# Chunk-select attention into soft mixture of experts: the first pair's loads, the last weight and the output stores rearranged

## The chip, the core and the metric

The kernel runs on one core of a Trainium2 chip. The metric is the device time of one execution in microseconds, the median of three runs. A separate profiled execution gives the trace; its own time stands beside its span below.

The core has a matrix engine (PE, TensorE), a vector engine (DVE), a scalar engine (ACT), GpSimd (POOL) and SyncE (SP). Each works through its own instructions in the order in which the program lists them, and waits on semaphores for the others. Transfers are issued by GpSimd or SyncE here and carried out by 16 DMA engines.

## What is computed

Two stages, with B = 4, H = 8, S = 768, D = 64 (the reference, cut):

```python
# attention that keeps, for each query row, 6 of 24 chunks of 32 keys
k_min, k_max = k_chunks.min(3), k_chunks.max(3)
ub = sum(maximum(q * k_min, q * k_max), -1)          # bound per chunk
ub = where(causal, ub, -1e9)
sel = chunk of the key is among the top 6 of ub
attn = softmax(where(sel & causal, q @ k.T / 8, -1e9))
x = (attn @ v) as (3072, 512)

# soft mixture of experts: 8 experts of 4 slots, F = 1024
logits = x @ phi                                      # (3072, 32)
slot_input = softmax(logits, over rows).T @ x         # (32, 512)
slot_out[e] = relu(slot_input[e] @ w1[e]) @ w2[e]
out = softmax(logits, over slots) @ slot_out          # (3072, 512), fp32
```

## The kernel before

**Units of work.** The attention is done in 16 pairs of heads (4 per batch element), each of 768 rows. One pair goes through these helpers: `load` (line 140) brings k and q, 192 KB each in bf16, by a GpSimd DMA that casts from the fp32 in memory; `load_v` (147) does the same for v. `transposes` (199) turns k or q with 12 small matmuls into a PSUM tile, which `evac_T` (211) copies out by ScalarE as kT or qT. `kmin` and `kmax` (220, 226) reduce the chunks on VectorE, `qsplit` (236) makes the negative and positive parts of q (for pair 0 the positive part is a ScalarE relu, line 241), `ubound` (246) multiplies them into the chunk bounds, and `select` (263) finds the sixth largest bound and marks the chunks below it (`ns`, not selected; one small copy by GpSimd at line 270). `ns_transposes` and `evac_ns` turn the marks. `scores` (290) then accumulates kT x qT and, from the constant `smask` and the turned marks, a large negative penalty; `expo` (314) is ScalarE's exponential, six per pair; `mask` (327) clears the causal triangle on GpSimd; `pv` (336) multiplies with v, and `normalise` (354) divides into x. `x_transposes` and `evac_x` turn x for the logits.

**The experts' side.** After every fourth pair (one batch element) the `moe_` helpers (385 to 496) compute logits with phi, a running maximum over rows, the dispatch product accumulated in `si_acc`, and the combine weights, kept turned in `cT_all`. The 16 weights of 1 MB in bf16 (w1 of expert e is number e, w2 is 8 + e) come by `load_w` (130), one GpSimd DMA each, cast from fp32. `wplan` (508) says in which pair's iteration `weights` (511) issues how many; number 0 is issued at 546, number 15 in the iteration of pair 15.

**Order.** There is no planner: each engine does its work in the order in which the lines are written, and the tile pools hand out buffers in rotation and insert the waits. PSUM tiles come from three pools with the tags "sc", "tp" and "at".

**The start** (156 to 192 and 517 to 568). VectorE clears constants, GpSimd issues k and q of pair 0, builds the identity, then builds `squad`, loads pair 1, builds `qgrp` and `caus`, and loads pair 2. VectorE adds `schunk` from `squad` (187) and ScalarE expands it to `smask` (188). PE runs `warm` (194), matmuls of 512 columns on ones whose result nobody reads: 9 before the transposes of the first k, 3 before those of q, then 2, 2 and 5. Pair 0's scores follow. phi and the second identity `identf` (fp32) are issued at 544 and 545 on GpSimd, ahead of weight 0. The loop over the other pairs is at 570; in it k and q of pair i + 4 are loaded at 595, v of pair i + 2 at 622, and the weights by 624 (or 575 for later ones, whose pools open there).

**The end.** GpSimd clears `siT_pad` and `hT_pad` (689, 690) and sets `zrow` (740) to ones. The slot sums are added into `siT_pad` and `zrow` on VectorE (743, 750). `experts_in` (762) and `relu` (772) give the hidden layer, `hidden_T` (775) turns it, `sums` (784) inverts the sums. `experts_out` (795) multiplies with w2 into two PSUM tiles, one for each column half y of 256; expert 7, the last weight, comes last: 8 matmuls for y = 0, then ScalarE's scaled copy `so_sb0` (847), 4 for y = 1, `half_out(0, 0)`, 4 more, and `so_sb1` (851), also ScalarE. The output is 12 row pairs m of 256 rows (two rows per partition, x = 0 and 1). `half_out` (827) does the first two row pairs by column halves: a product into a PSUM tile of its own for each x, `scaled` (821) by VectorE for x = 0 and by ScalarE for x = 1, and SyncE stores of 128, 128, 256, 256 and 256 KB, in which each partition's row piece has 1 KB. The loop at 857 does row pairs 2 to 11 whole (rows m of both x: 4 KB per partition, 512 KB per store, the last in two of 256 KB). Its PSUM tiles are separate for x = 0 and x = 1 and rotate over "at, sc, tp, sc, tp", and its five `o_sb` buffers are freed by the stores.

## Time and profile before

| | us |
|---|---|
| median of 3 runs | 166.47 (165.97 to 166.54) |
| profiled execution, its own time | 166.89 |
| its span in the trace | 165.2 |
| PE busy | 142.8 (86%) |
| ScalarE busy | 122.8 (74%) |
| VectorE busy | 119.9 (73%) |
| GpSimd busy | 103.1 (62%) |

The DMA engines moved 32.94 MB in the span, 199 GB/s on the mean. Besides, the exponentials of line 321 (96 of them, 83.1 us) are the largest group of ScalarE and the causal masks of line 331 (96, 38.4 us) that of GpSimd.

How to read what follows. The timeline lists runs of instructions on one engine: start, duration in us, engine, source line, operation, output<-inputs and shape, count, and in brackets the idle time before it with what ended that. PEld is PE's weight load. The page's rows by 40 slices give a busy share in tenths per slice, or the GB/s moved. A DMA row gives the size and the us from issue to landing. A row of waits names the waiting engine, line and tile, what it waited for, and total us, number of times and the longest. "Before" and "after" are times from the start of the span.

### The profile page before, as it was taken

To read this page: it belongs to the slowest core of one execution; us is meant where nothing else is said; L and a number is where in the kernel's file an instruction comes from. 1 tells how busy PE (TensorE), PEld (TensorE's weight loads), DVE (VectorE), ACT (ScalarE), POOL (GpSimd) and SP (SyncE) were. 2 spreads that over 40 slices of the span, in tenths; PEclk is the share of its full clock that TensorE was granted. 3 is DMA by queue.
4 is the path that set the end of the run, shared out by engine and by line. 5 is a ranking of instruction groups with operands and counts; after the bars stand their busy time and mean duration, and the time that the engine had idled before them with its cause. 6 is when DMAs were issued, how large, how long until landed. Compare 5 with 4: busy or idle time off the path is not lost.

```text
span 165.2 us, 6132 instructions
## 1 busy us (share of the span) xinstructions
PE 142.8 (86%) x2541; PEld 97.6 (59%) x2541; DVE 119.9 (73%) x419; ACT 122.8 (74%) x166; POOL 103.1 (62%) x202
## 2 busy tenths in 40 slices
PE   7986779999999898999999899998989999894500
PEld 2353456766767585677768567675868747552200
DVE  3376988989999979989997999898536521083620
ACT  3668879999999798999989699996886311193510
POOL 6978749979889398878949796768936200000000
PEclk9999999999999999999999999999999999999655
DMA  3999999999999999999999999999999999158995
GB/s 46 148 157 171 207 157 106 171 192 201 203 200 204 201 205 181 211 193 183 209 191 212 193 214 193 208 219 197 203 207 217 211 215 192 28 195 326 408 404 197
DMA packets 41132, 32.94 MB, mean 199 GB/s; under 512 B 26384, under 2 KB 35600, under 8 KB 41104
## 3 DMA queue, kind: packets, MB, share of 16 engines
q0 software_dynamic: 38416, 26.25, 108.0%
q1 hardware_dynamic: 2688, 6.29, 9.9%
q8 instruction: 20, 0.33, 0.7%
q14 instruction: 8, 0.07, 0.1%
HBM read 52.49 MB, written 6.29 MB: 356 GB/s over the span
## 4 chain that ended last, share of the span: by engine, by line
PE 31%; DMA 29%; ACT 18%; DVE 9%; issue 5%; POOL 4%; DVEq 0%; ACTq 0%
DMA w_sb<-in_moe_w_dram 14%; ACT e_sb L321 11%; DMA k_in<-in_k_dram 9%; DMA out_dram<-o_sb 6%; PE sc_ps L297 6%; PE at_ps L349 4%; PE tr_ps L205 4%; PE sc_ps L307 4%; PE warm_ps L197 4%; ACT qT L214 4%; PE xT_ps L371 2%; DVE mx L268 2%; PE ub_ps L256 2%; DVE x_sb L362 1%; POOL e_sb L331 1%
## 5 line engine op out<-in xcount | busy, mean ns | idle before, releaser
L321 ACT ACTIVATE e_sb<-sc_ps 128x1024 bf16<-128x1024 f32 (+1 forms) x96 | 83.1, 917 | 8.1 <-PE sc_ps L307 7.7
L331 POOL TENSOR_SCALAR_AFFINE_SELECT e_sb<-e_sb 128x256 bf16<-128x256 bf16 x96 | 38.4, 419 | 16.2 <-ACT e_sb L321 15.6
L297 PE MATMUL sc_ps<-qT,kT 64*128 64x384 bf16 (+3 forms) x258 | 36.8, 305 | 2.7 <-ACT e_sb L321 1.7
L307 PE MATMUL sc_ps<-nsT,smask 64*128 64x384 bf16 (+2 forms) x294 | 38.1, 284 | 0.1
L349 PE MATMUL at_ps<-v_t,e_sb 128*128 128x65 bf16 x672 | 29.9, 194 | 1.2 <-DVE x_sb L362 1.0
L349 PEld LDWEIGHTS <-e_sb 128*128 128x128 bf16 x672 | 25.4, 98 | 3.6 <-issue 2.1
L268 DVE MAX8 mx<-ub_ps 128x8 f32<-128x8 f32 (+1 forms) x192 | 17.0, 165 | 4.9 <-PE ub_ps L256 4.1
L297 PEld LDWEIGHTS <-kT 64*128 64x128 bf16 x258 | 14.0, 93 | 10.8 <-issue 5.4
L150 POOL DMA_DIRECT2D v_t<-in_v_dram x16 | 16.9, 1053 | 0.7 <-PE ns_ps L279 0.5
L307 PEld LDWEIGHTS <-smask 64*128 64x128 bf16 x294 | 14.9, 94 | 3.8 <-issue 0.6
L223 DVE TENSOR_REDUCE mm<-kT 128x24 bf16<-128x768 bf16 x16 | 15.1, 943 | 2.5 <-ACT kT L214 2.5
L362 DVE TENSOR_TENSOR x_sb<-at_ps,inv 128x768 bf16<-128x768 f32 (+1 forms) x17 | 15.5, 910 | 0.6
L229 DVE TENSOR_REDUCE mm<-kT 128x24 bf16<-128x768 bf16 x16 | 15.1, 943 | 0.0
L214 ACT COPY qT<-tr_ps 128x768 bf16<-128x768 bf16 x16 | 12.8, 800 | 2.5 <-PE tr_ps L205 2.5
L214 ACT COPY kT<-tr_ps 128x768 bf16<-128x768 bf16 x16 | 12.8, 801 | 1.5 <-PE tr_ps L205 1.5
L145 POOL DMA_DIRECT2D k_in<-in_k_dram x16 | 11.7, 734 | 1.1 <-POOLq L885 0.8
L145 POOL DMA_DIRECT2D q_in<-in_q_dram x16 | 11.5, 722 | 0.0
L138 POOL DMA_DIRECT2D w_sb<-in_moe_w_dram x16 | 11.4, 716 | 0.0
L382 DVE COPY xT_sb<-xT_ps 128x768 bf16<-128x768 bf16 (+1 forms) x15 | 8.1, 537 | 3.2 <-PE xT_ps L371 3.2
L863 PE MATMUL o_ps<-so_sb,cT_all 128*128 128x256 bf16 x40 | 6.8, 298 | 3.8 <-DVE o_sb L823 3.5
L205 PE MATMUL tr_ps<-ident,k_in 128*64 128x128 bf16 x192 | 8.7, 229 | 1.1 <-DMA k_in<-in_k_dram 1.1
L256 PE MATMUL ub_ps<-bd,qpn 128*128 128x48 bf16 x192 | 7.8, 183 | 1.3 <-DVE qpn L239 0.9
(125 smaller groups left out, 212.1 us busy)
## 6 DMA issues: line engine op xcount, KB each, us to landing
w_sb<-in_moe_w_dram POOLq DMA_DIRECT2D x16, 1024.0 KB, 14.0
out_dram<-o_sb SPq DMA_DIRECT2D x9, 512.0 KB, 5.3
k_in<-in_k_dram POOLq DMA_DIRECT2D x16, 192.0 KB, 7.0
q_in<-in_q_dram POOLq DMA_DIRECT2D x16, 192.0 KB, 7.3
v_t<-in_v_dram POOLq DMA_DIRECT2D x16, 192.0 KB, 8.5
out_dram<-oh_sb SPq DMA_DIRECT2D x3, 256.0 KB, 4.2
out_dram<-o_sb SPq DMA_DIRECT2D x2, 256.0 KB, 4.8
out_dram<-oh_sb SPq DMA_DIRECT2D x2, 128.0 KB, 1.9
```

The source lines that it names most:

```text
L145: nc.gpsimd.dma_start(out=t, in_=src.rearrange("h (p g) d -> p h (g d)", p=P))
L150: nc.gpsimd.dma_start(out=v_t[i % NV][:, :, :, :D], in_=v[b, 2 * j:2 * j + 2].rearrange("h (g p) d -> p h g d", p=P),)
L205: nc.tensor.matmul(ps[h * 64:(h + 1) * 64, g, :], lhsT=src[:, h, g * D:(g + 1) * D], rhs=ident, is_transpose=True,)
L214: nc.scalar.copy(t.rearrange("d (p g) -> d p g", g=NQT), st.pop((nm + "ps", i)).rearrange("d g p -> d p g"),)
L223: nc.vector.tensor_reduce(mm[:, 0, 0, :], kT, axis=AX.X, op=ALU.min)
L268: nc.vector.max(mx[:, a, :], ub[:, a, :max(8, 4 * t + 4)])
L297: nc.tensor.matmul(ps[:, h, c:c + w], lhsT=kT[r, kg * P:(kg + 1) * P], rhs=qT[r, qs], start=True, stop=False,)
L307: nc.tensor.matmul(ps[:, h, c + (f - t0) * P:c + (l - t0) * P], lhsT=smask[r, x, kg].rearrange("p a b -> p (a b)"), rhs=nsT[r, (f - x * NJ ...
L321: nc.scalar.activation(e[:, :, :w], st.pop(("scps", i, g))[:, :, :w], func=ACT.Exp, scale=scale)
L331: nc.gpsimd.affine_select(out=e[:, :, c:c + P], in_=e[:, :, c:c + P], compare_op=ALU.is_ge, fill=0.0, base=0, pattern=[[0, 2], [1, P]], ch ...
L349: nc.tensor.matmul(o, lhsT=st["e", i, g][:, h, c:c + P], rhs=v_t[i % NV][:, h, kg, :], start=(kg == 0), stop=(kg == t),)
L362: nc.vector.tensor_tensor(st["x", b][:, t0:t1, 2 * j:2 * j + 2, :].rearrange("p t h d -> p h t d"), at[:, :, :, :D], inv.broadcast_to([P, ...
```

## The change

**The start.** k and q of pair 0 are loaded by SyncE as fp32 into a `stage` tile (768 KB together, borrowed from the x pool), as the first thing in the program. A new `cast` converts each of them by halves: head 0 by VectorE, head 1 by ScalarE. GpSimd builds the identity first, then issues pair 1's k and q ahead of the constants. The warm matmuls become 5 and 1 instead of 9 and 3 (2, 2 and 5 stay). VectorE's `schunk` moves behind the cast of q, ScalarE's `smask` behind the relu of `qsplit(0)`, that is, behind kT and qT of pair 0 and ahead of kT of pair 1.

**The middle.** The second weight (w1 of expert 1) is issued before the loop, at `weights(0)`, which did nothing, instead of in the iteration of pair 1; the entry of pair 1 goes. The issue of phi and `identf` move into the iteration of pair 1, behind `load_v`.

**The end.** Weight 15 is taken out of the plan and issued after the loop, when the pads' tiles are allotted, in four DMAs of 256 KB, each covering two of the eight row groups fg of that weight. `experts_out` takes a list of fg; expert 7's 16 matmuls go quarter by quarter, each for y = 0 and y = 1, so that both halves end together. `so_sb0` is then scaled by ScalarE and `so_sb1` by VectorE. Only row pair 0 is stored by halves (128, 128 and 256 KB); all four of its products come first. Row pairs 1 to 11 are stored whole. Their PSUM tiles rotate over "at, sc, tp, sc": in "at" and "sc" x = 0 and x = 1 are the two banks of one tile `o2_ps`, in "tp" they are two tiles.

```diff
--- before.py
+++ after.py
@@ -129,6 +129,13 @@
 
     def load_w(i):
 
+        if i == 2 * E - 1:
+            src = moe_w2[E - 1].rearrange("(a p x) d -> p a (x d)", p=P, x=4)
+            dst = w_sb[i].rearrange("p (a f) -> p a f", a=NFG // 4)
+            for n in range(NFG // 2):
+                c = slice(n % 2 * 2 * Dm, (n % 2 + 1) * 2 * Dm)
+                nc.gpsimd.dma_start(out=dst[:, n // 2, c], in_=src[:, n // 2, c])
+            return
         if i < E:
             src = moe_w1[i].rearrange("(a p x) f -> p a (x f)", p=P, x=2)
             dst = w_sb[i].rearrange("p (a f) -> p a f", a=NDG // 2)
@@ -153,10 +160,13 @@
         )
 
 
+    stage = xp.tile([P, 2, 2, NQT * D], F32, name="stage", tag="x_sb")
+    for n, src in enumerate((k, q)):
+        nc.sync.dma_start(out=stage[:, n], in_=src[0, :2].rearrange("h (p g) d -> p h (g d)", p=P))
     nc.vector.memset(ones_sq, 1.0)
-    load(0, "k")
-    load(0, "q")
     make_identity(nc, ident)
+    load(1, "k")
+    load(1, "q")
     for t in (squad, caus, qgrp, headsel, ns_t[0], ns_t[1], c_pad):
         nc.vector.memset(t, 0.0)
     for t in v_t:
@@ -172,8 +182,6 @@
         out=squad, in_=squad, compare_op=ALU.not_equal, fill=-1.0, base=-NCHUNK,
         pattern=[[-CH, 2], [-64, 2], [0, NCHUNK]], channel_multiplier=1,
     )
-    load(1, "k")
-    load(1, "q")
     nc.gpsimd.affine_select(
         out=qgrp, in_=qgrp, compare_op=ALU.not_equal, fill=1.0, base=0,
         pattern=[[-1, 4], [0, CH]], channel_multiplier=1,
@@ -184,11 +192,6 @@
     )
     load(2, "k")
     load(2, "q")
-    nc.vector.tensor_tensor(schunk[:, :, :, 0], squad[:, :, 0, :], squad[:, :, 1, :], op=ALU.add)
-    nc.scalar.copy(
-        smask.rearrange("p o t a x -> p (o t a) x"),
-        schunk.rearrange("p o c x -> p (o c) x").broadcast_to([P, 2 * NCHUNK, CH]),
-    )
     warm_ps = p_at.tile([P, 4, P], F32, name="warm_ps", tag="at")
 
     def warm(n):
@@ -505,7 +508,7 @@
             step(i // NPB)
 
 
-    wplan = {1: 1, 2: 1, 3: 1, 4: 1, 6: 1, 8: 1, 9: 1, 10: 1, 11: 2, 12: 1, 13: 2, 14: 1, 15: 1}
+    wplan = {0: 1, 2: 1, 3: 1, 4: 1, 6: 1, 8: 1, 9: 1, 10: 1, 11: 2, 12: 1, 13: 2, 14: 1}
     nw = 1
 
     def weights(i):
@@ -514,15 +517,27 @@
             load_w(nw)
             nw += 1
 
-    warm(9)
+    def cast(n, nm):
+        t = st[nm, 0] = inp.tile([P, 2, NQT * D], BF16, name=nm + "_in", tag=nm + "_in")
+        nc.vector.tensor_copy(t[:, 0], stage[:, n, 0])
+        nc.scalar.copy(t[:, 1], stage[:, n, 1])
+
+    warm(5)
+    cast(0, "k")
     transposes(0, "k")
+    cast(1, "q")
     evac_T(0, "k")
+    nc.vector.tensor_tensor(schunk[:, :, :, 0], squad[:, :, 0, :], squad[:, :, 1, :], op=ALU.add)
     kmin(0)
     kmax(0)
-    warm(3)
+    warm(1)
     transposes(0, "q")
     evac_T(0, "q")
     qsplit(0)
+    nc.scalar.copy(
+        smask.rearrange("p o t a x -> p (o t a) x"),
+        schunk.rearrange("p o c x -> p (o c) x").broadcast_to([P, 2 * NCHUNK, CH]),
+    )
     warm(2)
     transposes(1, "k")
     evac_T(1, "k")
@@ -541,8 +556,6 @@
     kmin(1)
     kmax(1)
     qsplit(1)
-    nc.gpsimd.dma_start(out=phi_sb, in_=moe_phi.rearrange("(hg p) s -> p hg s", p=P))
-    make_identity(nc, identf)
     load_w(0)
 
     for g in range(5):
@@ -622,6 +635,9 @@
             load_v(i + 2)
         if i < EARLY:
             weights(i)
+        if i == 1:
+            nc.gpsimd.dma_start(out=phi_sb, in_=moe_phi.rearrange("(hg p) s -> p hg s", p=P))
+            make_identity(nc, identf)
         scores(i, 4)
         expo(i, 4)
         if i == LAST:
@@ -650,6 +666,7 @@
     pads = ctx.enter_context(tc.tile_pool(name="pads", bufs=1))
     siT_pad = pads.tile([P, NDG, E, CH], BF16, name="siT_pad")
     hT_pad = pads.tile([P, NFG, E, CH], BF16, name="hT_pad")
+    load_w(2 * E - 1)
     BL = B - 1
     normalise(LAST - 1)
     pv(LAST, [0, 1, 2])
@@ -792,9 +809,9 @@
     so_t = p_at.tile([P, 2, 512], F32, name="so_ps0", tag="at")
     so_ps = [so_t[:, 0, :HD], p_sc.tile([P, HD], F32, name="so_ps1", tag="sc")]
 
-    def experts_out(fs, es, ys):
-        for y, f in ((y, f) for y in ys for f in fs):
-            for fg in range(f * 4, (f + 1) * 4):
+    def experts_out(fgs, es, ys):
+        for y in ys:
+            for fg in fgs:
                 for e in es:
                     g, j = divmod(e, 4)
                     nc.tensor.matmul(
@@ -811,9 +828,8 @@
     hidden_T(0)
     experts_in(1, 1)
     relu(1)
-    NM, NH = B * NQT // 2, 2
-    homes = {"sc": p_sc, "tp": p_tp, "at": p_at}
-    half_homes = [iter("tp at sc tp".split()), iter("sc tp sc tp".split())]
+    NM = B * NQT // 2
+    homes = {"sc": p_sc, "at": p_at}
 
     def rows(m):
         return out[m * 2 * P:(m + 1) * 2 * P, :].rearrange("(p x) d -> p x d", x=2)
@@ -824,46 +840,49 @@
         else:
             nc.scalar.activation(o, ps, func=ACT.Copy, scale=cinv(n))
 
-    def half_out(m, y):
-        o_sb = op.tile([P, 2, HD], F32, name="oh_sb", tag="oh_sb", bufs=2 * NH)
-        for x in range(2):
-            tag = next(half_homes[y])
-            o_ps = homes[tag].tile([P, HD], F32, name="oh_ps", tag=tag)
-            nc.tensor.matmul(o_ps, lhsT=cT[:, m, x], rhs=so_sb[y], start=True, stop=True)
-            scaled(x, o_sb[:, x, :], o_ps, 2 * m + x)
-            if m == y == 0:
-                nc.sync.dma_start(out=rows(m)[:, x, :HD], in_=o_sb[:, x, :])
-        if m + y > 0:
-            nc.sync.dma_start(out=rows(m)[:, :, y * HD:(y + 1) * HD], in_=o_sb)
+    def product(ps, m, x, y):
+        nc.tensor.matmul(ps, lhsT=cT[:, m, x], rhs=so_sb[y], start=True, stop=True)
 
     w_ctx.close()
     op = ctx.enter_context(tc.tile_pool(name="op", bufs=5))
-    experts_out([0], range(4), [0, 1])
+    f0, f1 = range(NFG // 2), range(NFG // 2, NFG)
+    experts_out(f0, range(4), [0, 1])
     hidden_T(1)
     sums()
-    experts_out([1], range(4), [0, 1])
-    experts_out([0, 1], [4, 5, 6], [0, 1])
-    experts_out([0, 1], [7], [0])
+    experts_out(f1, range(4), [0, 1])
+    experts_out(range(NFG), [4, 5, 6], [0, 1])
+    for n in range(NFG // 2):
+        experts_out(range(2 * n, 2 * n + 2), [7], [0, 1])
     nc.scalar.activation(so_sb[0], so_ps[0], func=ACT.Copy, scale=zinv)
-    experts_out([0], [7], [1])
-    half_out(0, 0)
-    experts_out([1], [7], [1])
-    nc.scalar.activation(so_sb[1], so_ps[1], func=ACT.Copy, scale=zinv)
-    half_out(1, 0)
-    for m in range(NH):
-        half_out(m, 1)
-
-    n = 0
-    for m in range(NH, NM):
+    nc.vector.tensor_scalar_mul(so_sb[1], so_ps[1], zinv)
+
+    heads = [[p_tp.tile([P, HD], F32, name="oh_ps", tag="tp") for x in range(2)]]
+    h_sc = p_sc.tile([P, 2, 512], F32, name="oh2_ps", tag="sc")
+    heads.append([h_sc[:, x, :HD] for x in range(2)])
+    for y in range(2):
+        for x in range(2):
+            product(heads[y][x], 0, x, y)
+    for y in range(2):
+        o_sb = op.tile([P, 2, HD], F32, name="oh_sb", tag="oh_sb", bufs=2)
+        for x in range(2):
+            scaled(x, o_sb[:, x, :], heads[y][x], x)
+            if y == 0:
+                nc.sync.dma_start(out=rows(0)[:, x, :HD], in_=o_sb[:, x, :])
+        if y > 0:
+            nc.sync.dma_start(out=rows(0)[:, :, HD:], in_=o_sb)
+
+    for m in range(1, NM):
+        tag = ("at", "sc", "tp", "sc")[(m - 1) % 4]
+        if tag == "tp":
+            o_ps = [p_tp.tile([P, Dm], F32, name="o_ps", tag="tp") for x in range(2)]
+        else:
+            t = homes[tag].tile([P, 2, 512], F32, name="o2_ps", tag=tag)
+            o_ps = [t[:, x, :] for x in range(2)]
         o_sb = op.tile([P, 2, Dm], F32, name="o_sb", tag="o_sb")
         for x in range(2):
-            tag = ("at", "sc", "tp", "sc", "tp")[n % 5]
-            o_ps = homes[tag].tile([P, Dm], F32, name="o_ps", tag=tag)
             for y in range(2):
-                nc.tensor.matmul(
-                    o_ps[:, y * HD:(y + 1) * HD], lhsT=cT[:, m, x], rhs=so_sb[y], start=True, stop=True)
-            scaled(x, o_sb[:, x, :], o_ps, 2 * m + x)
-            n += 1
+                product(o_ps[x][:, y * HD:(y + 1) * HD], m, x, y)
+            scaled(x, o_sb[:, x, :], o_ps[x], 2 * m + x)
             if m == NM - 1:
                 nc.sync.dma_start(out=rows(m)[:, x], in_=o_sb[:, x, :])
         if m < NM - 1:
```

## The prediction

> **What bounds the kernel now.** I read the chain of waits first, because this kernel has a different limit in each stretch, then the timeline of both ends, then the waits and DMA rows between them.
>
> The start, from the timeline (start, duration, engine, line, operation):
>
> ```profile
> 0.90 0.17 DVE L156 MEMSET ones_sq<- 128x128 bf16 x1 [0.90 <-PEq L885]
> 1.12 4.02 PE L197 MATMUL warm_ps<-ones_sq 128*128 128x512 bf16 x9 [1.12 <-DVE squad L161]
> 4.30 1.47 ACT L188 COPY smask<-schunk 128x1536 bf16<-128x1536 bf16 x1 [2.22 <-DVE schunk L187]
> 5.08 0.85 PE L205 MATMUL tr_ps<-ident,k_in 128*64 128x128 bf16 x12
> 5.86 1.32 PE L197 MATMUL warm_ps<-ones_sq 128*128 128x512 bf16 x3
> 5.97 0.80 ACT L214 COPY kT<-tr_ps 128x768 bf16<-128x768 bf16 x1 [0.20 <-PE tr_ps L205]
> 7.68 0.80 ACT L214 COPY qT<-tr_ps 128x768 bf16<-128x768 bf16 x1 [0.91 <-PE tr_ps L205]
> 8.51 0.84 ACT L241 ACTIVATE qpn<-qT 128x768 bf16<-128x768 bf16 x1
> 9.26 0.78 ACT L214 COPY kT<-tr_ps 128x768 bf16<-128x768 bf16 x1
> 10.09 0.53 PE L205 MATMUL tr_ps<-ident,q_in 128*64 128x128 bf16 x12 [0.23 <-ACT kT L214]
> 10.55 1.25 PE L197 MATMUL warm_ps<-ones_sq 128*128 128x512 bf16 x5
> 11.64 0.33 PE L279 MATMUL ns_ps<-ident,ns_t 128*128 128x128 bf16 x3
> 12.85 3.35 ACT L321 ACTIVATE e_sb<-sc_ps 128x1024 bf16<-128x1024 f32 x4 [1.40 <-PE sc_ps L307]
> ```
>
> The first exponential starts at 12.85. Back from it runs a chain through PE's five warm matmuls and the second q transposes to ScalarE's copy of the second kT, which ends at 10.04. So ScalarE, not the arrival of k, is late here. The smask copy sits before the first kT, where ScalarE had nothing to do.
>
> After that ScalarE is busy for 8 or 9 tenths of nearly every slice up to 120 us (the page's row by 40 slices, below), so a delay of the first exponential moves everything behind it. At the end two things meet (a row of the chain, then the timeline):
>
> ```profile
> ACT  3668879999999798999989699996886311193510
> ...
> 119.00 23.35 DMA w_sb<-in_moe_w_dram
> ...
> 138.91 2.80 PE L800 MATMUL so_ps<-w_sb,hT_pad 128*32 128x256 bf16 x80
> 142.40 1.47 PE L800 MATMUL so_ps<-w_sb,hT_pad 128*32 128x256 bf16 x12 [0.69 <-DMA w_sb<-in_moe_w_dram]
> 143.47 0.47 ACT L847 ACTIVATE so_sb<-so_ps,inv_b 128x256 bf16<-128x256 f32 x1 [5.61 <-PE so_ps L800]
> 144.30 0.61 PE L800 MATMUL so_ps<-w_sb,hT_pad 128*32 128x256 bf16 x4
> 144.86 0.85 SPq L835 DMA_DIRECT2D out_dram<-oh_sb  x2
> ```
>
> PE has done its work by 141.71 and waits only 0.69 us for the last weight, though the chain shows a DMA of 23.35 us there. From 144.86 the stores decide. Their rates, in 40 slices of the stretch 144 to 166 (0.55 us each):
>
> ```profile
> GB/s 0 0 0 237 240 130 344 356 333 244 17 411 406 417 395 387 425 402 402 417 387 425 387 402 395 417 410 365 439 387 425 410 354 399 291 26 4 0 0 0
> ```
>
> **The change, part by part.** All sums are made in the profiled execution (166.89 us, of which the span is 165.2) and carried over to the median of the three runs, 166.47.
>
> *k and q through SyncE.* No row shows an fp32 load on SyncE's queue. The nearest:
>
> ```profile
> k_in<-in_k_dram POOLq DMA_DIRECT2D x1, 192.0 KB, 3.4
> q_in<-in_q_dram POOLq DMA_DIRECT2D x1, 192.0 KB, 4.1
> out_dram<-oh_sb SPq DMA_DIRECT2D x2, 128.0 KB, 1.9
> 127.83 0.48 ACT L382 COPY xT_sb<-xT_ps 128x384 bf16<-128x384 bf16 x1 [0.83 <-PE xT_ps L371]
> ```
>
> The fp32 k is 384 KB. SyncE's 128 KB take 1.9 us; 256 KB more at the 400 GB/s of the rate row add 0.65. GpSimd's load, which reads the same 384 KB, took 3.4. Issued as SyncE's first work, at about 0.9 like VectorE's first memset, k lands between 3.45 and 4.3; I take 3.5. The q behind it lands at 4.4 if it has the DMA engines to itself, at 5.6 if k and q of pair 1, now issued by GpSimd ahead of the constants, take half of them; I take 5.0. The Trainium skill ("DMA: Bandwidth & Descriptors", Queues, rings and completion order) says that each engine takes turns between the queues that have work, which speaks for the later end; by it the start would be worse by 0.6 us. No row shows two queues loading at once.
>
> Each half cast costs about 0.5 (the 128x384 row above), on VectorE and ScalarE side by side. But ScalarE casts its half of q before it copies kT, so kT starts at about 5.5, only 0.45 sooner than now. Behind it now stand, without a gap: kT to 6.3, qT at 6.4 (its transposes start at 5.55 and take 0.85) to 7.2, relu to 8.0, **smask, 1.47**, to 9.45, second kT to 10.2. It ended at 10.04 before. The gap that smask filled is gone, and smask is on the path: **+0.2** us. With q at 4.4 it is -0.4, with q at 5.6 +0.8. VectorE's two casts and the later schunk lie ahead of kmin, which waits for kT anyhow.
>
> *Second weight, phi and identity.* GpSimd issues the second weight right behind v of pair 2, at about 21 instead of 27.84. The rows: rates in 40 slices from 4 to 30 (0.65 us each), the two issues, the waits between 14 and 44 and between 44 and 70 (total, times, longest), and one copy:
>
> ```profile
> GB/s 170 161 51 135 194 196 118 197 199 169 71 149 178 176 158 156 171 161 176 207 211 202 208 214 214 186 196 149 163 155 160 121 31 27 61 196 200 127 123 161
> 20.14 1.05 POOL L150 DMA_DIRECT2D v_t<-in_v_dram  x1
> 27.84 0.70 POOL L138 DMA_DIRECT2D w_sb<-in_moe_w_dram  x1
> POOL ns_t L270 <- DVE mx L268: 2.7, 2, 1.6
> PEld L205 <- DMA k_in<-in_k_dram: 1.1, 2, 0.6
> 56.62 0.80 ACT L214 COPY kT<-tr_ps 128x768 bf16<-128x768 bf16 x1 [0.37 <-PE tr_ps L205]
> ```
>
> The weight fills the hole in the loads: the three slices 31, 27 and 61 lose about 1.4 us against the 200 around them. All later loads move up by at least that, and the two waits of PE for k between 44 and 70 (0.6 and 0.5 us, of which the first leaves ScalarE idle for 0.37) end: **-0.5**, between 0 and -0.7. The k of pair 5 falls behind the weight but has slack. Phi's issue and the identity move to pair 1, behind v of pair 3; GpSimd stands waiting for 2.7 us in that part, which hides them, and they are first read in the iterations of pairs 5 and 6. Without that cover their 1.3 us would hold back masks that the next pair reads.
>
> *Last weight in quarters.* It is now issued after pair 15's masks:
>
> ```profile
> 119.00 0.77 POOL L138 DMA_DIRECT2D w_sb<-in_moe_w_dram  x1
> 126.10 0.94 POOL L689 MEMSET siT_pad<- 128x1024 bf16 x1
> 128.74 0.19 POOL L740 MEMSET zrow<- 1x128 f32 x1
> 132.28 0.35 DVE L743 TENSOR_TENSOR siT_pad<-si_acc,si_ps 128x64 bf16<-128x64 f32 x2 [0.44 <-PE si_ps L474]
> 132.55 0.23 DVE L750 TENSOR_TENSOR zrow<-si_acc,si_ps 1x16 f32<-1x16 f32 x2
> ```
>
> Four issues of 0.72 hold the memsets back by 2.9: siT_pad is clear at 129.9 and zrow at 131.9, needed at 132.28 and 132.55. Hidden, with 0.7 to spare for zrow. The loads have a backlog of 16 us at 126.1, so the queue doesn't run dry. The weight lands earlier than PE wants it, and the 0.69 us go. But now all 16 of its matmuls stand ahead of the first so_sb, not 8. The 12 in 1.47 give 0.11 each behind a first of 0.27: 16 take 1.9 instead of 1.05, that is **+0.85 for -0.7**. First store: 141.7 + 1.9 + the 1.4 from PE's end to 144.86 = 145.0, against 144.86: **+0.1**.
>
> *Whole rows.* Two of the three 256 KB stores of half rows become one of whole rows. Against 405 GB/s the eight slices from 237 to 17 lose 1339 GB/s-slices x 0.55 us = 0.74 MB, or 1.8 us. The first three stores stay and keep the first four slices' 0.9 of that; 0.9 could be won. What speaks against it is in the program: both halves x of a row pair now share one PSUM tile, and the x = 1 matmuls wait until VectorE has read x = 0, ScalarE again for both. The two engines worked side by side before; now they go in turns. The price of a turn:
>
> ```profile
> 152.65 0.75 DVE L823 TENSOR_SCALAR o_sb<-o_ps,inv_a 128x512 f32<-128x512 f32 x1 [2.70 <-DMA out_dram<-o_sb]
> 153.46 0.82 PE L863 MATMUL o_ps<-so_sb,cT_all 128*128 128x256 bf16 x4 [2.85 <-DVE o_sb L823]
> 151.00:152.00 1.00, 0.00 (x0) 0.00 (x0) 0.00 (x0) 0.00 (x0) 0.00 (x0) 1.00 1.01 406
> 154.00:156.00 2.00, 1.34 (x7) 0.60 (x6) 1.39 (x2) 1.25 (x2) 0.00 (x0) 0.50 1.02 408
> ```
>
> VectorE 0.75, then four matmuls 0.61 (144.30), with the release of 0.06: 1.4 us for 512 KB, but 0.75 where every fourth pair has tiles of its own: 1.25 on average against 1.3 in the stores. It just keeps up, and the first 512 KB go out at about 147.2. The two window rows hold, after the stretch and its length, the busy time and count of PE, PEld, DVE, ACT and POOL, the granted clock, the DMA share and GB/s. At the granted clock of 0.50, which PE shows from 154 on after a stretch with no matmul at all (151 to 152), a turn costs about 1.9 and the average 1.6. I take **-0.2**, between -0.9 and +1.2.
>
> **Sum:** +0.2 - 0.5 + 0.1 - 0.2 = -0.4: 166.47 - 0.4 = 166.0 (rounded).
>
> **The rivals.**
>
> *Slower: PE's clock rises late at the start.* The nine warm matmuls took 0.45 us each, the three at 5.86 0.44, the five at 10.55 0.25: PE got faster in between, after standing busy almost without a break from 1.12 to 7.2. Now six warm matmuls fewer run, with PE idle from about 3.3 to 4.0 and again before q. If the faster clock has not come by 10.2, the five cost 2.1 (+0.9), the q transposes 0.85 (+0.3), and ns_ps and the first scores about twice their 0.7 (+0.5): +1.7 on the path; with the forecast's -0.4 that is +1.3, or 167.8. It decides if PE isn't busy enough between 5.5 and 9.4, where q's transposes, two warm matmuls, the second k's transposes, two more and the bounds stand almost without a gap; that speaks against it, the gaps ahead of them for it. The Trainium skill ("TensorE: Matmul & The Clock Gate", Part 1: The HAM clock gate) has the clock rise after a window of about 3.4 us of sustained work that runs free of the kernel; the trace agrees in that the rise came only after two such windows of warm matmuls. By that rule it is a matter of phase. **0.22.**
>
> *Faster: q lands by 4.4 and the stores keep up.* The start is then -0.4, the middle -0.5 as in the forecast, the meeting +0.1, and the stores win 0.8 of the possible 0.9: -1.6, or 164.9. For it: the 1.9 us row, and the turns' average of 1.25 against 1.3; against it: pair 1's loads at the same time. **0.28.**
>
> *The stores become bound by the turns* at the half clock: start and middle as forecast, stores +0.8: 167.1. For it: PE works a third of the time there, and the clock is 0.50 there in the kernel before; against it: it held 1.00 to 152, after a pause. **0.1.**
>
> *The forecast*, 165.3 to 166.8: **0.4.**
>
> **How the numbers follow.** A measurement of this kernel tells about 0.5% (0.83 us) from no change. Faster: 0.26 of the fast rival, 0.08 of the forecast's lower end: 0.34. Slower: 0.2 of the clock and 0.04 of the turns: 0.24. Same is the rest, 0.42. The range from 164.7 to 167.9 takes in both rivals.
>
> **What would show it.** The second kT copy of ScalarE ending near 10.2 and the first exponential near 13.1 (14.5 under the clock rival, with five warm matmuls in 2.1 us). No wait of the transposes for k_in in 44 to 70, and no wait of PE for w_sb. First store near 145.0. VectorE and ScalarE in turns after 146, with o_sb starts 1.4 apart. I am wrong if GpSimd's four issues make siT_pad late, or if q waits beyond 5.6.

## The result, and the profile after

The changed kernel is slower: 170.72 us median of four runs (170.03 to 171.18) against 166.5 of the kernel before, a ratio of 1.0261 with a 95% interval of 1.0211 to 1.0310. The forecast was 166.0, the range 164.7 to 167.9. The profiled execution took 170.71 with a span of 169.0 (166.89 and 165.2 before). Some executions of a kernel were disturbed, over 1.5% above its fastest: the ratios leave these out, the medians and ranges in the table below do not, and the profiled executions of e4_last, f2_shared and h1_warm7 were such ones, so their traces are not read.

The 3.8 us of the span can be followed along the timeline, first the start (start, duration, engine, line, operation):

```profile
4.27 0.91 PE L208 MATMUL tr_ps<-ident,k_in 128*64 128x128 bf16 x12 [0.84 <-DVE k_in L522]
5.22 0.51 ACT L523 CAST q_in<-stage 128x384 bf16<-128x384 f32 x1 [0.94 <-DMA stage<-in_q_dram]
5.64 0.79 ACT L217 COPY kT<-tr_ps 128x768 bf16<-128x768 bf16 x1
8.25 1.45 ACT L537 COPY smask<-schunk 128x1536 bf16<-128x1536 bf16 x1
9.61 0.79 ACT L217 COPY kT<-tr_ps 128x768 bf16<-128x768 bf16 x1
10.91 1.25 PE L200 MATMUL warm_ps<-ones_sq 128*128 128x512 bf16 x5
12.00 0.33 PE L282 MATMUL ns_ps<-ident,ns_t 128*128 128x128 bf16 x3
13.21 1.02 ACT L324 ACTIVATE e_sb<-sc_ps 128x1024 bf16<-128x1024 f32 x1 [1.40 <-PE sc_ps L310]
```

k arrived early enough for the transposes at 4.27 (5.08 before), but smask stands ahead of the second kT, which ends at 10.40. The first exponential starts at 13.21: **0.36 late**. The five warm matmuls take 1.25, so PE had its fast clock by then (it rose at 7.6; at 6.9 in the kernel before).

Then pair 1 and pair 2, the same view:

```profile
21.52 0.72 POOL L145 DMA_DIRECT2D w_sb<-in_moe_w_dram  x1
28.53 0.76 POOL L639 DMA_DIRECT2D phi_sb<-in_moe_phi_dram  x1
29.27 0.23 POOL masks.py:197 MEMSET identf<- 128x128 f32 x1
29.58 0.29 POOL masks.py:199 TENSOR_SCALAR_AFFINE_SELECT identf<-identf 128x128 f32<-128x128 f32 x1
29.83 1.49 POOL L334 TENSOR_SCALAR_AFFINE_SELECT e_sb<-e_sb 128x256 bf16<-128x256 bf16 x4
30.65 0.46 PE L352 MATMUL at_ps<-v_t,e_sb 128*128 128x65 bf16 x9 [0.64 <-POOL e_sb L334]
31.64 1.51 ACT L324 ACTIVATE e_sb<-sc_ps 128x768 bf16<-128x768 f32 x2 [0.85 <-PE sc_ps L310]
```

phi and identf hold four masks back to 29.83. PE waits 0.64 for one of them and ScalarE 0.85 for the scores behind it. The same two rows in the kernel before:

```profile
28.54 1.49 POOL L331 TENSOR_SCALAR_AFFINE_SELECT e_sb<-e_sb 128x256 bf16<-128x256 bf16 x4
30.37 1.51 ACT L321 ACTIVATE e_sb<-sc_ps 128x768 bf16<-128x768 f32 x2 [0.15 <-PE sc_ps L307]
```

The exponential that started at 30.37 starts at 31.64. It is 1.27 late: the 0.36, 0.21 that appear with the weight's issue at 21.52, and **0.70 more**. Later the two waits for k end, which gives 0.53 back, and the last exponential is 0.59 late.

The end, with the waits of the last weight and the row pairs:

```profile
139.50 3.25 PE L817 MATMUL so_ps<-w_sb,hT_pad 128*32 128x256 bf16 x88
143.38 0.60 PE L817 MATMUL so_ps<-w_sb,hT_pad 128*32 128x256 bf16 x4 [0.63 <-DMA w_sb<-in_moe_w_dram]
144.62 0.60 PE L817 MATMUL so_ps<-w_sb,hT_pad 128*32 128x256 bf16 x4 [0.65 <-DMA w_sb<-in_moe_w_dram]
146.45 0.83 SPq L870 DMA_DIRECT2D out_dram<-oh_sb  x2
151.95 1.01 PE L844 MATMUL o_ps<-so_sb,cT_all 128*128 128x256 bf16 x4 [0.84 <-DVE o_sb L839]
152.57 0.69 ACT L841 ACTIVATE o_sb<-o_ps,inv_a 128x512 f32<-128x512 f32 x1 [1.17 <-PE o_ps L844]
153.00 0.75 DVE L839 TENSOR_SCALAR o_sb<-o_ps,inv_a 128x512 f32<-128x512 f32 x1 [1.10 <-PE o_ps L844]
153.80 1.01 PE L844 MATMUL o_ps<-so_sb,cT_all 128*128 128x256 bf16 x4 [0.84 <-DVE o_sb L839]
```

PE waits for the last two quarters, 1.28 in all where it waited 0.69 before, and the first store goes out at 146.45, **1.59 late** (144.86 before). From there every engine waits for the next one: PE for VectorE, ScalarE and VectorE for PE, a turn of 1.85 to 1.92 us per row pair on a shared tile, 1.62 on the mean with every fourth pair, which has two tiles. The clock shows it too (windows: length, then PE, PEld, DVE, ACT, POOL, granted clock, DMA share, GB/s), and so do the rates of 144 to 169 in 40 slices:

```profile
147.00:149.00 2.00, 0.94 (x4) 0.54 (x4) 0.97 (x2) 0.94 (x2) 0.00 (x0) 0.64 0.57 197
149.00:151.00 2.00, 1.76 (x8) 1.13 (x8) 0.90 (x2) 0.97 (x2) 0.00 (x0) 0.50 0.83 327
155.00:160.00 5.00, 2.87 (x12) 1.68 (x12) 2.58 (x4) 2.17 (x4) 0.00 (x0) 0.50 0.77 315
```

```profile
GB/s 3 0 0 0 0 205 215 211 267 406 374 79 393 413 413 374 334 380 118 360 419 79 354 380 420 406 295 400 282 157 400 295 105 406 380 387 377 23 0 0
```

The clock is 0.50 from 147.6 on, where before it held 1.00 to 153.7. The stores have gaps (79, 118, 79, 105 GB/s) in which no row pair is ready. From the first store to the end: 22.5 us against 20.3, **2.2 lost**.

### The profile page after: what moved, and what is told of

The parts are those of the page before. It is cut to its first block, busy times and chain, and to the rows that moved or that the text cites. A ratio compares the mean times of both kernels' runs of the same rounds, so it can differ in the third digit from the quotient of the medians.

```text
span 169.0 us, 6109 instructions
## 1 busy us (share of the span) xinstructions
PE 144.0 (85%) x2535; PEld 98.7 (58%) x2535; DVE 121.8 (72%) x421; ACT 123.4 (73%) x166; POOL 102.7 (61%) x203
## 4 chain that ended last, share of the span: by engine, by line
PE 41%; ACT 17%; DMA 11%; DVE 11%; POOL 9%; issue 6%; POOLq 0%; DVEq 0%; ACTq 0%
ACT e_sb L324 11%; DMA w_sb<-in_moe_w_dram 10%; PE sc_ps L300 7%; PE at_ps L352 7%; PE o_ps L844 6%; PE sc_ps L310 5%; PE tr_ps L208 5%; DVE o_sb L839 4%; PE xT_ps L374 3%; ACT qT L217 3%; POOL e_sb L334 2%; DVE x_sb L365 2%; DMA stage<-in_k_dram 2%; PE ub_ps L259 1%; DVE mx L271 1%
## 5 line engine op out<-in xcount | busy, mean ns | idle before, releaser
L352 PE MATMUL at_ps<-v_t,e_sb 128*128 128x65 bf16 x672 | 29.9, 194 | 2.2 <-DVE x_sb L365 1.4
L844 PE MATMUL o_ps<-so_sb,cT_all 128*128 128x256 bf16 x44 | 10.5, 401 | 7.2 <-DVE o_sb L839 7.2
L844 PEld LDWEIGHTS <-cT_all 128*128 128x128 bf16 x48 | 6.4, 133 | 11.9 <-issue 9.8
L152 POOL DMA_DIRECT2D k_in<-in_k_dram x15 | 11.0, 735 | 0.4 <-issue 0.3
L152 POOL DMA_DIRECT2D q_in<-in_q_dram x15 | 10.8, 720 | 0.4 <-issue 0.4
L145 POOL DMA_DIRECT2D w_sb<-in_moe_w_dram x15 | 10.6, 712 | 0.0
L841 ACT ACTIVATE o_sb<-o_ps,inv_a 128x512 f32<-128x512 f32 x8 | 5.5, 687 | 7.0 <-PE o_ps L844 7.0
```

The source lines that it names most:

```text
L152: nc.gpsimd.dma_start(out=t, in_=src.rearrange("h (p g) d -> p h (g d)", p=P))
L352: nc.tensor.matmul(o, lhsT=st["e", i, g][:, h, c:c + P], rhs=v_t[i % NV][:, h, kg, :], start=(kg == 0), stop=(kg == t),)
L844: nc.tensor.matmul(ps, lhsT=cT[:, m, x], rhs=so_sb[y], start=True, stop=True)
```

## The experiments

A theory of three separate faults, each tested by undoing it: the shared PSUM tiles in turns (2.2 us), phi and identf in pair 1 (0.7), and the last weight that lands no sooner although the second is issued sooner. The main rival in each case is that the end was bound elsewhere. All ratios are to the kernel before, run beside each kernel.

| kernel | median us (range, runs) | ratio (interval) |
|---|---|---|
| e3_split | 168.17 (167.03-169.83, 10) | 1.0072 (1.0023-1.0120) |
| f1_split_phi | 166.92 (166.03-168.88, 10) | 0.9981 (0.9938-1.0024) |
| f2_shared | 169.03 (167.07-171.69, 10) | 1.0051 (0.9999-1.0102) |
| g1_plan_shared | 168.30 (166.94-169.03, 10) | 1.0066 (1.0028-1.0103) |
| e2_w1 | 168.38 (166.57-170.37, 10) | 1.0045 (0.9996-1.0095) |
| e4_last | 172.08 (168.67-177.16, 4) | none |
| f3_plan | 165.66 (164.67-166.91, 10) | 0.9924 (0.9875-0.9973) |
| h3_after_again | 170.71 (169.68-171.09, 4) | 1.0169 (1.0116-1.0222) |
| e1_start | 169.17 (167.80-169.81, 4) | 1.0103 (1.0034-1.0171) |
| h2_start_again | 168.18 (167.24-169.56, 12) | 1.0051 (1.0014-1.0087) |
| f4_smask | 169.31 (168.25-170.34, 4) | 1.0141 (1.0043-1.0238) |
| h1_warm7 | 168.08 (166.44-170.67, 12) | 1.0007 (0.9963-1.0051) |
| g2_plan_split | 167.75 (166.56-168.99, 10) | 1.0014 (0.9971-1.0058) |
| g3_plan_split_oldstart | 166.35 (165.50-168.34, 10) | 0.9954 (0.9914-0.9994) |
| h4_plan_start7 | 166.16 (164.79-167.54, 12) | 0.9881 (0.9844-0.9918) |

### The stores

**e3_split**, in the changed kernel:

```diff
-        tag = ("at", "sc", "tp", "sc")[(m - 1) % 4]
...
-            o_ps = [t[:, x, :] for x in range(2)]
+        tags = [("at", "sc", "tp", "sc", "tp")[(2 * m - 2 + x) % 5] for x in range(2)]
+        o_ps = [homes[tag].tile([P, Dm], F32, name="o_ps", tag=tag) for tag in tags]
```

> The changed kernel with the whole row pairs' products in five PSUM tiles, one for each x, as before, and nothing else. My theory: the 2.2 us lost from the first store to the end are the turns of VectorE, PE and ScalarE on a shared two-bank tile, at PE's half clock 1.86 each; with tiles of their own PE fills the next while the others read, the stores set the pace again (1.3 us per 512 KB), and the time falls by 2 to 2.5 us to about 168.4. Rival, the half clock of PE or the stores themselves are the limit: the time stays within 0.5 us of 170.7.

The ratio fell from 1.0261 to 1.0072; run once more, the changed kernel had 1.0169 (h3_after_again), so the gain is 1.0 to 1.9%. Its timeline, and a window as above:

```profile
154.34 0.69 ACT L841 ACTIVATE o_sb<-o_ps,inv_a 128x512 f32<-128x512 f32 x1 [0.56 <-DMA out_dram<-o_sb]
154.36 0.75 DVE L839 TENSOR_SCALAR o_sb<-o_ps,inv_a 128x512 f32<-128x512 f32 x1 [0.50 <-DMA out_dram<-o_sb]
155.16 1.01 PE L844 MATMUL o_ps<-so_sb,cT_all 128*128 128x256 bf16 x4 [0.24 <-DVE o_sb L839]
```

```profile
155.00:160.00 5.00, 1.59 (x6) 0.65 (x5) 2.36 (x4) 2.09 (x4) 0.00 (x0) 0.50 1.02 405
```

VectorE and ScalarE now start together and wait for the stores' buffers, and the stores run at 405 GB/s although the clock is 0.50 and four matmuls still take 1.01. So the half clock alone is not the limit; on the shared tiles it is. First store to end: 20.3 (145.10 to 165.4), as in the kernel before, so the whole rows themselves win nothing in this trace. The last weight happened to be in time in this execution, so the first store shows that part too.

**f2_shared** does one part alone: the same shared tiles for row pairs 2 to 11 of the kernel before, the reverse of the diff above.

> The kernel before with the shared two-bank PSUM tiles alone, for row pairs 2 to 11. My theory: turns of 1.4 us at PE's full clock (1.25 on average) keep up with the stores, turns of 1.86 (1.62 on average) behind the fall of the clock don't; with the clock falling at 150 to 154 some 6 to 8 row pairs lose 0.3 each: +1.5 to +2.5 us, all of it after the first store. Rival, the loss of the changed kernel came from its late first store and the idle PE ahead of it, not from the shared tiles: within 0.5 us of the kernel before.

It costs about 0.5% (0.8 us), less than I expected; the interval just touches no loss. Over all ten executions the median lies 1.65 us above that of the kernel before beside it (169.03 against 167.38), which is in the range expected, so the size of this part alone stays uncertain. **g1_plan_shared** and **g2_plan_split** carry the other mends (below) and differ in the tiles alone:

> The changed kernel with phi and the identity back ahead of weight 0 and weights 5 to 10 issued one iteration sooner, the shared PSUM tiles kept. The last weight should now be in before PE wants it, so PE has no idle time ahead of the first store (about 143.7). If the shared tiles cost by themselves: the clock falls some 8 us behind the first store, from then on turns average 1.6 us against 1.3, and first store to end takes 21 to 22 us: 165.5 to 166.5 in all. If they cost only together with the late weight (which brought the clock down ahead of the first whole row pair): first store to end takes 20.3 as in e3_split, 164.7 in all, no different from g2_plan_split.

Shared is slower by 0.5% (1.0066 against 1.0014; the intervals overlap). The spans of the two traces differ by 1.2 us (166.4 and 165.3), but 0.8 of that lies ahead of the first store: in g1's trace the clock was 0.50 from 22.9 to 26.3, and the exponentials fell back by 1.2 us there, which is far ahead of the shared tiles. Later PE had no wait for the last weight, a turn took 1.44 us while the clock was 1.00, and first store to end took 20.8 (145.68 to 166.4), not 22.5:

```profile
150.23 0.60 PE L843 MATMUL o_ps<-so_sb,cT_all 128*128 128x256 bf16 x4 [1.06 <-DVE o_sb L838]
151.67 0.60 PE L843 MATMUL o_ps<-so_sb,cT_all 128*128 128x256 bf16 x4 [0.84 <-DVE o_sb L838]
155.94 1.01 PE L843 MATMUL o_ps<-so_sb,cT_all 128*128 128x256 bf16 x4 [0.90 <-DVE o_sb L838]
```

So on the shared tiles the end took 0.4 us longer than with separate ones where the clock fell at 152.6 (20.8 here, 20.4 in g2_plan_split), and 1.8 to 2.2 longer than e3_split's 20.3 where it fell at 149.4 (22.2, h3_after_again) and 147.6 (22.5, the changed kernel).

What brings the clock down is not shown in full, but a wait for the last weight is not needed for it, and 1.5 us of waiting is not enough. These are windows of 3.41 us: the one ahead of the fall in the changed kernel, the one ahead of the fall in h3_after_again, and one of e1_start (below):

```profile
144.16:147.57 3.41, 1.53 (x12) 1.05 (x11) 2.02 (x4) 1.42 (x3) 0.00 (x0) 1.00 0.07 24
146.02:149.43 3.41, 1.47 (x11) 1.01 (x11) 2.50 (x5) 1.64 (x3) 0.00 (x0) 1.00 0.32 110
141.44:144.85 3.41, 1.75 (x22) 1.18 (x13) 0.00 (x0) 0.47 (x1) 0.00 (x0) 1.00 0.03 6
```

In h3_after_again the last wait for the weight was over at 145.11. In the window that follows, PE stood idle for VectorE's turns (1.07 and 0.84), was busy for 1.47 of 3.41 us, and the clock fell at its end. In e1_start PE waited longer for the weight (1.53 in one piece), was busy for 1.75, and the clock held until 155.1. So the turns leave PE idle enough for the fall without the late weight.

### phi, and the last weight

**f1_split_phi** is e3_split with this undone:

```diff
-        if i == 1:
-            nc.gpsimd.dma_start(out=phi_sb, in_=moe_phi.rearrange("(hg p) s -> p hg s", p=P))
-            make_identity(nc, identf)
...
     qsplit(1)
+    nc.gpsimd.dma_start(out=phi_sb, in_=moe_phi.rearrange("(hg p) s -> p hg s", p=P))
+    make_identity(nc, identf)
     load_w(0)
```

> The changed kernel with separate PSUM tiles per x, as in e3_split, and with phi's load and the fp32 identity back ahead of weight 0. My theory: GpSimd's 1.3 us for these two in pair 1 hold back four masks, and ScalarE then waits 0.85 for scores before pair 2's third exponential; the lag of the exponentials against the kernel before, +0.7 from there on, goes to about +0.1, and the time falls by 0.5 to 0.7 against e3_split, to within 0.5 us of the kernel before. Rival, the end is set by the last weight's landing and not by the exponentials: no change against e3_split (ratio to before about 1.007).

The ratio is 0.9981, within 0.5 us of the kernel before as expected, and 0.9% under e3_split, which is more than expected. In the trace the masks go at once, and the exponential that was 1.27 late is 0.33 late and follows without a gap, so the 0.70 is gone:

```profile
28.40 1.19 POOL L334 TENSOR_SCALAR_AFFINE_SELECT e_sb<-e_sb 128x256 bf16<-128x256 bf16 x3
30.70 1.51 ACT L324 ACTIVATE e_sb<-sc_ps 128x768 bf16<-128x768 f32 x2
```

With two faults undone the change is worth nothing either way. For the third, **e2_w1** takes one part alone into the kernel before, `wplan = {0: 1, 2: 1, ...}` instead of `{1: 1, 2: 1, ...}`:

> The kernel before with the second weight alone issued sooner (ahead of the loop). My theory: PE's two waits for k between 44 and 70 go (-0.6 us by the exponentials there), at the cost of some 0.2 for a mask behind the issue. But with the hole in the loads filled the DMA engines never come to an even start again, and if that is what made one engine so late in the changed kernel, the last weight lands at 143 or later and the first store is no sooner than before: 166 to 167. Rival, the late engine comes from the quarters or from their place: the last weight lands at 141.5 to 142 and the end moves by -0.4.

In its trace the weight's issue makes the exponentials 0.23 later, and the end of the waits for k 0.53 sooner, as in the changed kernel. But the last weight's matmuls waited until 143.33 (142.40 before), and the time did not fall. Where did the earlier loads go? The rates between 56 and 80 us (0.6 us a slice), of before, e2_w1 and the changed kernel in turn:

```profile
GB/s 220 214 215 220 212 212 187 194 220 185 174 169 181 190 197 179 172 207 201 220 221 201 212 218 205 199 201 189 195 177 197 167 185 194 182 177 191 157 220 215
DMA packets 9151, 4.72 MB, mean 197 GB/s; under 512 B 6533, under 2 KB 8591, under 8 KB 9147
```

```profile
GB/s 218 215 188 191 186 183 182 126 136 169 184 191 167 163 192 214 207 205 225 198 218 198 186 192 192 198 173 155 158 168 168 168 146 124 151 131 167 191 157 212
DMA packets 8884, 4.32 MB, mean 180 GB/s; under 512 B 6368, under 2 KB 8416, under 8 KB 8880
```

```profile
GB/s 232 212 212 209 184 203 198 184 177 162 107 144 176 200 164 149 180 195 202 212 218 212 212 184 206 173 202 197 174 167 169 148 177 161 145 141 141 155 195 206
DMA packets 8886, 4.37 MB, mean 182 GB/s; under 512 B 6360, under 2 KB 8408, under 8 KB 8881
```

Where the second weight comes sooner, two new holes open at about 62 and 76 us, and 0.35 to 0.40 MB less are moved. The queue has caught up with the program there: the next loads are not issued before their pair's iteration. **f3_plan** puts weights into these holes:

```diff
-    wplan = {1: 1, 2: 1, 3: 1, 4: 1, 6: 1, 8: 1, 9: 1, 10: 1, 11: 2, 12: 1, 13: 2, 14: 1, 15: 1}
+    wplan = {0: 1, 2: 1, 3: 1, 4: 1, 5: 1, 7: 1, 8: 1, 9: 1, 10: 1, 11: 1, 12: 1, 13: 2, 14: 1, 15: 1}
```

> The kernel before with a plan that issues the second weight ahead of the loop and weights 5 to 10 one iteration sooner. My theory: the gain of 2.6 us in the landings that the second weight sooner gave up to weight 4 was lost where the queue ran dry again, at about 60 to 62 and 72 to 74 us (pair 10's k landed 3.1 us after its issue there). With weights issued into these gaps the gain is kept: the last weight's median engine lands at 138 to 139 instead of 141.0, PE doesn't wait for it, and the first store goes out at about 143.7 instead of 144.86: -0.8 to -1.3 us. Rival, the last landings follow the pace of the loop or one late engine whatever the plan: median engine at 140.3 to 141 as with the second weight alone, time as before or up to +1.

The rival is out: 0.9924, faster than before (the interval ends at 0.9973). The landing marks in the traces (16 for a transfer, one of each DMA engine; median, and for the last weight also the last mark):

| us | before | e2_w1 | changed | f3_plan |
|---|---|---|---|---|
| second weight | 36.1 | 29.9 | 30.5 | 30.4 |
| weight number 4 | 60.7 | 57.9 | 59.2 | 58.6 |
| weight number 6 | 84.0 | 83.1 | 84.1 | 78.4 |
| last weight (last quarter) | 141.4 | 140.6 | 141.3 | 138.9 |
| its last mark | 142.4 | 143.3 | 144.6 | 140.2 |

At weight 4 a lead of 1.5 to 2.7 us is left, and at weight 6 it is 0.9 or nothing, unless the holes are filled. In f3_plan PE's matmuls run through, and the first store goes out at 143.28:

```profile
138.59 3.69 PE L800 MATMUL so_ps<-w_sb,hT_pad 128*32 128x256 bf16 x92
143.28 0.85 SPq L835 DMA_DIRECT2D out_dram<-oh_sb  x2
```

The second part of the lateness is one or two engines that are behind the others: 3.3 us between the median and the last mark in the changed kernel (2.5 to the mark before the last), 1.0 before. **e4_last** (the last weight whole, at its old place) and **h3_after_again** (the changed kernel once more) asked where that comes from.

> The changed kernel with the last weight in one DMA issued in pair 15's iteration, as before; its matmuls stay in the new order. If the quarters or their late issue made it late: it lands by 142.5, PE's idle time before the last matmuls shrinks, first store at about 145.3 against 146.45, the time about 1 us less, 169.6. If the DMA engines were already apart before it (second weight sooner, start): it lands at about 144.2 as now, all 16 matmuls come after that instead of 4, and the time is 171.5 to 172.

> The changed kernel once more. If the late engine of its profile (last landing 2.8 us behind the median one) is scatter, as 1.2 us in e3_split with the same loads suggests, another profile shows 1 to 2.5; if it comes each time, 2.5 to 3 again. The turns on the shared tiles should be there in either case: first store to end 21.5 to 22.6 us, and the ratio to before at 1.018 to 1.028.

e4_last scattered from 168.67 to 177.16 and settles nothing. The changed kernel had 2.5 the second time and PE waited 0.52 and 0.63 again; first store to end was 22.2, as expected, and the ratio, 1.0169, a little under its range. But e3_split and f1_split_phi, with the last weight loaded in the same way, had 1.2 and 1.1, and h4_plan_start7, whose last weight is whole, 2.5. So the quarters aren't shown to be the cause; what makes one engine late stays open.

### The start

**e1_start** and the same kernel again, **h2_start_again**: the start part alone in the kernel before.

> The kernel before with the start part alone (fp32 k and q by SyncE, casts, 5 and 1 warm matmuls, smask behind the relu of q). My theory: smask, 1.45 us on ScalarE, now stands on the path to the first exponential, which starts at 13.2 instead of 12.85, and the whole kernel is slower by that much and no more: +0.3 to +0.5 us. Rival, the start spreads the DMA engines apart and so makes the last weight late: the last weight's matmul waits beyond 143, first store after 145.5, +1 us or more.

> The same kernel as e1_start, for more executions beside h1_warm7. If the start costs only what its first exponential shows: ratio to before 1.002 to 1.004. If the 1.0 per cent of e1_start stands: 1.008 to 1.014.

The first exponential started at 13.09 in e1's trace and at 13.22 in h2's, near the 13.2 expected. The 1.0% did not stand, but the cost, 0.5% (0.1 to 0.9), is more than the delay of 0.24 and 0.38 us would be. In the traces that delay is not what costs: it is gone from 57 us on, where the kernel before waits for k, and at the last exponential e1 is level with the kernel before and h2 0.15 us ahead. What is late is the last weight, which is e1's rival (in the kernel before it is the row at 142.40; here e1, then h2):

```profile
143.23 1.47 PE L808 MATMUL so_ps<-w_sb,hT_pad 128*32 128x256 bf16 x12 [1.53 <-DMA w_sb<-in_moe_w_dram]
143.40 1.47 PE L808 MATMUL so_ps<-w_sb,hT_pad 128*32 128x256 bf16 x12 [1.85 <-DMA w_sb<-in_moe_w_dram]
```

The first store goes out at 145.69 and 145.86, 0.8 and 1.0 late. The median landing mark is where it was (141.5 and 141.4), the last one 1.7 and 2.0 us behind it. Whether the start makes that engine late is not shown: e3_split and f1_split_phi have the same start and 1.2 and 1.1. **f4_smask** moves smask behind the second kT, **h1_warm7** puts 7 warm matmuls where the start part has 5:

> The kernel before with the start part alone, as in e1_start, but with the smask copy one place later, behind the second kT instead of ahead of it. My theory: smask is all that the start lost; the second kT then ends at about 9.0 instead of 10.4, and the first exponential starts at 12.4 to 12.6 instead of 13.2 (12.85 before): -0.3 us against before, -0.7 against e1_start. Rival, the marks' chain on VectorE (kmin to ns_t, which ended at 11.2) or PE's five warm matmuls set the first exponential: it starts at 12.9 to 13.2 still.

> The start part alone as in e1_start, with 7 warm matmuls instead of 5 ahead of the first k's transposes, so that PE is busy without a gap until these. If the later rise of PE's clock is what the start costs: the clock rises by 7.9 at the latest, the first exponential starts at 12.8 to 13.1, and the time is 0.5 to 1 per cent below h2_start_again. If not (a cost behind the start, as a later last weight): the same as h2_start_again within 0.3 per cent.

f4 was a miss: the second kT ended at 9.44, yet the first exponential started at 13.23. In that execution PE stayed slow (start, duration):

```profile
7.74 0.85 PE L201 MATMUL tr_ps<-ident,k_in 128*64 128x128 bf16 x12
8.53 1.03 PE L193 MATMUL warm_ps<-ones_sq 128*128 128x512 bf16 x2
10.21 0.78 PE L201 MATMUL tr_ps<-ident,q_in 128*64 128x128 bf16 x12
```

The same two warm matmuls took 0.60 at 8.01 in the changed kernel, and q's transposes 0.53 at 10.45. With 7 warm matmuls the ratio is 1.0007, but its interval overlaps that of h2, and the medians of all twelve executions of each differ by 0.1 us only (168.08 and 168.18). So it is not shown that fewer warm matmuls are the loss. **h4_plan_start7** has both edits on f3_plan:

> f3_plan with the start part, 7 warm matmuls and smask behind the second kT. If smask and the clock were what the start lost, the first exponential starts at 12.4 to 12.7 and the time is 0.2 to 0.4 us below f3_plan's ratio of 0.992, at 0.990. If the start part costs something else, it stays at 0.997 or above.

```profile
6.60 0.71 PE L193 MATMUL warm_ps<-ones_sq 128*128 128x512 bf16 x2
8.29 0.78 ACT L210 COPY kT<-tr_ps 128x768 bf16<-128x768 bf16 x1
12.62 1.94 ACT L317 ACTIVATE e_sb<-sc_ps 128x1024 bf16<-128x1024 f32 x2 [1.47 <-PE sc_ps L303]
```

The first exponential starts at 12.62 (12.74 in f3_plan's trace) and the first store at 143.20 (143.28), and 0.9881 (0.9844 to 0.9918) is the best of all, faster than both kernels; against f3_plan the intervals overlap. **g2_plan_split** and **g3_plan_split_oldstart** say the same of the start, and something of the whole rows:

> As g1_plan_shared, with separate PSUM tiles per x as in e3_split. All three faults that I see are then mended: first store at about 143.7, 20.3 us from there to the end, 164.5 to 165.2 in all, ratio to the kernel before 0.985 to 0.992. If the start part costs more than the 0.3 us of its first exponential (e1_start was 1.0 per cent slower), it is slower than g3_plan_split_oldstart by 0.7 us or more.

> As g2_plan_split, with the start of the kernel before (k and q of pair 0 by GpSimd in bf16, smask ahead of the first kT, 9 and 3 warm matmuls). By my theory the start part alone is worth +0.1 to +0.4 us, so this is 0.1 to 0.4 us faster than g2_plan_split. Against f3_plan, which has the tail of before, it shows what whole rows and the last weight in quarters are worth: within 0.5 us of its ratio of 0.992 if they are worth nothing, 0.987 if the 0.9 us that could be won by fewer half rows is won.

g2 missed its range. The old start is 0.6% faster than the new one with 5 warm matmuls, but the intervals overlap and the spans of the two traces are alike (165.4 and 165.3, with a clock of 0.50 from 22.9 to 26.3 in g3's as in g1's). And g3, with whole rows and quarters, is no better than f3_plan with the old tail (0.9954 against 0.9924): no gain of those parts is shown.

## Why the prediction was wrong, step by step

In the profiled executions the terms came out as follows: start +0.36 (forecast +0.2), weight, phi and identity +0.2 (-0.5), last weight +1.0 (+0.1), whole rows +2.2 (-0.2), in all +3.8 (-0.4).

- **"I take -0.2, between -0.9 and +1.2" (whole rows).** This step cost most. The mechanism was named and a turn priced rightly (1.4 at the full clock, 1.9 at the half: 1.44 and 1.85 measured), and as a rival it had a chance of 0.1 and a price of +0.8. What failed is the place of the clock's fall, which I left at 154, where the kernel before had it, 8.8 us behind its first store. On the shared tiles it came 1.1 us behind the first store (2.5 in h3_after_again), ahead of nearly all row pairs: +2.2. The rival had the reason at hand ("PE works a third of the time there") and set it aside because the clock of the kernel before held to 152; which share PE's wait for the last weight had in the fall is not shown. The Trainium skill ("TensorE: Matmul & The Clock Gate", HAM oscillation — how this bites in real kernels) describes a clock that falls in waits on a DMA of 3 to 5 us. In e2_w1 a wait of 2.10 was enough (it fell at 144.0), in e1_start and h2_start_again 1.53 and 1.85 were not, so the traces don't bear that chain out for the 0.63 and 0.65 here.
- **"GpSimd stands waiting for 2.7 us in that part, which hides them" (phi and the identity).** Wrong, by +0.7. The 2.7 were a sum over 14 to 44 us and lay ahead of the small copies of line 270, not behind load_v, where four masks followed without a gap (28.54 before). f1_split_phi shows the price.
- **"All later loads move up by at least that."** Wrong. The waits for k ended as forecast (0.53 for the 0.5; the hole itself is 1.6 us by its three slices, not 1.4), but the loads' lead was lost at 62 and 76 us, and the weight's issue cost 0.21 ahead of pair 1's masks, which I hadn't counted. "The loads have a backlog ... so the queue doesn't run dry" was true at 126 and not at 62.
- **"The weight lands earlier than PE wants it": +0.1.** Measured +1.0 beyond the lag of the loop, because the weight landed later and not earlier: PE waited 1.28 us for it instead of not at all. By the landing marks either cure would have been enough (an estimate): with f3_plan's median, 2.4 sooner, or with the spread of 1.0 of before, the last mark comes by 142.3, and PE wanted the third quarter at 142.75. Where the weight was in time (e3_split, f1_split_phi) the new order was cheaper than forecast: the first store came 0.24 after and 0.78 ahead of before's, with last exponentials 0.78 late and 0.18 early, so some -0.6.
- **The start, +0.2.** Right in its mechanism and nearly in size for this execution (0.36; second kT at 10.40 for 10.2, q in by 5.2 for 5.0, five warm matmuls in 1.25). In h3_after_again the first exponential was 0.93 late, with the clock up at 9.5 instead of 7.6. With the start alone (e1_start, h2_start_again) the delay was gone at the last exponential and a late last weight cost 0.8 and 1.0 in its place. The Trainium skill ("TensorE: Matmul & The Clock Gate", Part 1: The HAM clock gate) says that the number of slow matmuls varies from run to run; the rises at 7.6 and 9.5 in two executions of the changed kernel agree. The clock rival did not come to the 1.7 us that I priced.
- The sum took the clock of the kernel before for granted in a stage in which the change itself leaves PE idle, and the half clock raised the mean turn from the forecast's 1.25 to 1.62, above the 1.3 of the stores.

## What to carry to other kernels

Read a stall's cover at the place of the edit: an engine's waiting time summed over a stretch hides nothing unless it lies between the moved instruction and what waits behind it. A load that is issued sooner gains at the end only if the queue stays full from there on, so look at the rates of all later stretches and fill the holes that open. When producer and two readers share one PSUM tile, price the turn at the half clock, for the turns leave PE idle enough for the clock to fall.

## What the runs showed of the hardware that was not expected

The 16 landing marks of one 1 MB weight (of its last quarter, where it comes in quarters) lay 1.0 to 3.3 us apart between the median and the last, from execution to execution (before 1.0, e3_split 1.2, e1_start 1.7, e2_w1 2.7, changed 3.3 and 2.5), and PE waits for the last one.

In each trace the moments at which PE's clock changes lie whole multiples of 3.41 us apart (before: 6.91 and 153.68, 43 steps; changed: 7.62 and 147.57, 41 steps), and where these steps lie differs from execution to execution. In the 14 traces read, behind 130 us, the clock fell at the end of a step in which PE was busy for 0.48 of the time or less (0.45 in the changed kernel, 0.43 in h3_after_again, 0.48 in f4_smask), and held through those of 0.47 or more (0.47 in g1_plan_shared, 0.51 in e1_start). No idle stretch as long as a step was needed: the longest ahead of the fall was 1.07 us in the changed kernel.
